# Two-head bias attention with a bilinear FFN: the tail keys' weighted values as 64-row matmuls, one accumulator bank per head

## The chip, the cores and the metric

The kernel runs on one core of a Trainium2 chip. The metric is the device time of one execution in microseconds (us); lower is better. A core has five engines that work on their own instruction streams and wait for each other by semaphores: TensorE (PE in the profile; its weight loads are listed apart as PEld), VectorE (DVE), ScalarE (ACT), GpSimd (POOL) and SyncE (SP). Here POOL and SP do little but issue DMAs.

## What is computed

```python
# q, k, v: (8 batches, 8 heads, 576 positions, 64), bias_table: (32, 8)
scores = q @ k.T / 8 + bias[head, |i - j| bucket]
attn   = softmax(scores)
x      = attn @ v              # heads side by side: (8 * 576, 512)
out    = ((x @ w_a) * (x @ w_b)) @ w_out     # 512 -> 1536 -> 512
```

In the kernel the bias enters as a factor: exp(score) is multiplied by exp(bias), and the sum of the weights comes out of the same matmul as the values, since v carries a column of ones (65 columns for a head).

## The kernel before

**Pairs.** The 64 heads of all batches are handled as 32 pairs of neighbouring heads; pair p belongs to batch p // 4. The 576 positions are split into 512 (four tiles of 128) and a tail of 64. So the two heads' tails of 64 make one tile of 128 rows: rows 0 to 63 for the first head, 64 to 127 for the second.

**Scores.** `qk` computes key tiles against queries, transposed (keys on the partitions): for each of four key tiles one bank-pair tile `qk` with both heads' 512 queries, as two matmuls of 64 rows (the head dimension), one for each head. They go in two groups, t = 0, 1 and t = 2, 3. With the second group come the "rows": all four key tiles against the 64 tail queries, 64-row and 64-column matmuls (L424), the first head into the bank `trb`, the second into a bank `qr` of the pool `ps_av`. `qk_tail` computes the tail keys against all queries (`qkt`). ACT takes the exponentials (`ex`, L439; `ex_rows`, L431; `ex_tail`, L515), VectorE multiplies with the bias factors (`mul`, L444; `mul_rows`, L539; `mul_tail`, L531). `mul_tail` writes the last 256 columns of the tail weights `att`: those of query tile 3 and of the tail queries (tile 4). For tail keys against query tiles 0 to 2 the factor is constant and drops out.

**Weighted values.** `av(p, jqs)` accumulates, for query tiles jq, into one bank `av` of the pool `ps_av`, a slot of 2 x 65 columns for each tile: first the tail keys of both heads in one matmul of 128 rows and 130 columns (L568; `vt` has zeros where a head meets the other head's rows), then four key tiles for each head (L578, 65 columns each). Tile 4 (the tail queries of both heads) instead takes four matmuls of 130 columns (L572). `av_norm` divides on VectorE (`rc`, L589; L591; L596) into `XG`. The calls are `av(p, (0, 1, 2))` and `av(p, (3, 4))`, one after the other through the same bank, and between them in most steps the row scores use that bank. `t_x` then transposes `XG` into `xn` by two DMAs on SP's queue (L604, L607).

**FFN.** Token chunks of 512 go through units: `pa` (four matmuls of 512 columns, then ACT copies to `ha`, L649), `pb` (four matmuls, then VectorE multiplies with `ha` into `g`, L652), and `po` (three units of four matmuls each, L679; then ACT copies to `ob`, L684, and issues the output DMA). The units take turns in two banks (`ps_ff`): a pa's bank is free when its `ha` is written, a pb's when its `g` is, a po's when its `ob` is. A chunk has 24 pa and pb units in turn and 12 of po.

**Order.** Everything is written out by hand; each engine runs its instructions in program order, and semaphores follow from what is read and written. After an opening that handles the pairs 0 to 7, a loop over s = 8 to 32 (the last function printed below) does the scores of pair s and the weighted values of pair s − 1. Its list `steps` is a sequence of these calls with places `U`; at each `U` one FFN unit is put, nine in a step. A chunk is 36 units, that is four steps: in steps with s mod 4 = 1 the units are pa, pb, ... pa; with s mod 4 = 2 pb, pa, ... pb; with s mod 4 = 3 six pa and pb and three po; with s mod 4 = 0 nine po. In steps with s mod 4 = 0 `av(p, (3, 4))` stands before the second score group (`late` before `pair`), in the others after it. Every step ends with `mul_tail(s)` behind the ninth unit. In step 32 the last pair's values are computed without scores, and the remaining units follow with two more banks.

PSUM has eight banks: four for scores (`ps_sc`, two tiles of two), one for `ps_av`, one for `trb`, two for the FFN. `trb` serves the transposes of the opening in two halves (`tr_half`).

Of the kernel before, what the change touches and what calls it, by code (L numbers as in the profile page):

```python
# [13 lines left out]
def kernel(  # L14
# [11 lines left out]
    nc = tc.nc  # L26
    FP32 = mybir.dt.float32
    BF16 = mybir.dt.bfloat16
    ACTF = mybir.ActivationFunctionType
    MULT = mybir.AluOpType.mult  # L30

    B, H, S, Dh = 8, 8, 576, 64
    NB = 32
    NM = 4
    SM = 128 * NM
    ST = S - SM
# [11 lines left out]
    wrk = ctx.enter_context(tc.tile_pool(name="wrk", bufs=2))  # L48
    atp = ctx.enter_context(tc.tile_pool(name="atp", bufs=10))
    ps_sc = ctx.enter_context(tc.tile_pool(name="ps_sc", bufs=2, space=bass.MemoryType.PSUM))  # L50
    ps_av = ctx.enter_context(tc.tile_pool(name="ps_av", bufs=1, space=bass.MemoryType.PSUM))
    ps_tr = ctx.enter_context(tc.tile_pool(name="ps_tr", bufs=1, space=bass.MemoryType.PSUM))
# [45 lines left out]
    vm = [wpool.tile([128, H, NM, Dh + 1], BF16, name=f"vm{i}") for i in range(2)]  # L98
    vt = [wpool.tile([128, 2, H // 2, Dh + 1], BF16, name=f"vt{i}") for i in range(2)]
# [8 lines left out]
    XG = [wpool.tile([128, 5, 2, Dh], BF16, name=f"XG{i}") for i in range(2)]  # L108
# [116 lines left out]
    def load_first(x, dst):  # L225
# [8 lines left out]
                        in_=bass.AP(tensor=bias_table.tensor, offset=(NB - 1) * H,  # L234
                                    ap=[[0, NB], [1, H]]))
# [5 lines left out]
                            op=mybir.AluOpType.subtract)  # L241
    warm = ps_av.tile([128, 512], FP32, tag="av", name="warm")

    def warm_up(n, dst=None):
        for _ in range(n):
# [7 lines left out]
                     start=True, stop=True)  # L253
# [54 lines left out]

    st = [dict() for _ in range(NP)]

    trb = ps_tr.tile([128, 1024], BF16, tag="tr", name="trb")
    turn = [0]

    def tr_half():
        turn[0] ^= 1
        return trb[:, 512 * turn[0]:512 * turn[0] + 512]

    def copy(eng, out, in_):
        if eng is nc.scalar:
# [88 lines left out]
    def qk(p, t0, ts=None):  # L408
        qT, kT, _ = operands(p)
        st[p].setdefault("at", [None] * NM)  # L410
        for t in ts or (t0, t0 + 1):
            ps = ps_sc.tile([128, 2, 512], FP32, tag="sc", name=f"qk{p}_{t}")
            for hh in range(2):
                r = slice(64 * hh, 64 * hh + 64)
                nc.tensor.matmul(out=ps[:, hh, :], lhsT=kT[r, t, :], rhs=qT[r, :, :],  # L415
                                 start=True, stop=True)
            st[p]["ps", t] = ps
        if shared(p) and t0 == 2:
            z = operands(p)[2]
            rows = (trb.bitcast(FP32), ps_av.tile([128, 512], FP32, tag="av", name=f"qr{p}"))  # L420
            for t in range(NM):
                for hh in range(2):
                    r = slice(64 * hh, 64 * hh + 64)
                    nc.tensor.matmul(out=rows[hh][:, ST * t:ST * t + ST], lhsT=kT[r, t, :],  # L424
                                     rhs=z[r, 0, ST * hh:ST * hh + ST], start=True, stop=True)
            st[p]["rows"] = rows
# [9 lines left out]
    def ex(p, t):  # L436
        ps = st[p]["ps", t]
        at = atp.tile([128, 2, SM], BF16, tag="at", name=f"at{p}_{t}")
        nc.scalar.activation(out=at[:, :, :], in_=ps[:, :, :], func=ACTF.Exp, scale=scale)  # L439
        st[p]["at"][t] = at  # L440

    def mul(p, t):
        at, w = st[p]["at"][t], W_sb[p % 4]
        nc.vector.tensor_tensor(out=at[:, :, :], in0=at[:, :, :],  # L444
                                in1=w[:, :, S - 1 + t:S - 1 + t - SM:-1], op=MULT)
# [95 lines left out]
    def weights(p, t, hh, jq):  # L541
        if p >= 4:
            return st[p]["at"][t][:, hh, 128 * jq:128 * jq + 128]
        o = 256 * (t % 2) + 128 * (jq % 2)
        return st[p]["at", jq // 2, t // 2][:, hh, o:o + 128]

    def weights_last(p, t):
        return st[p]["att"][:, 2 * ST * t:2 * ST * t + 2 * ST]

    def weights_tail(p, jq):  # L550
        if jq == 4:
            o = 512 + main_tail(p)
            return st[p]["att"][:, o:o + 2 * ST]
        if p < 4 and jq < 2:
            return atk[:, p, 128 * jq:128 * jq + 128]
        o = 512 + 128 * (jq if p >= 4 else jq - 2)
        return st[p]["att"][:, o:o + 128]

    def av(p, jqs):
        av_mm(p, jqs)  # L560
        av_norm(p, jqs)

    def av_mm(p, jqs, pool=None, tag="av"):
        b, hp = divmod(p, 4)
        i = b % 2
        pav = (pool or ps_av).tile([128, 3, 2, Dh + 1], FP32, tag=tag, name=f"av{p}_{jqs[0]}")
        for slot, jq in enumerate(jqs):
            nc.tensor.matmul(out=pav[:, slot, :, :], lhsT=weights_tail(p, jq),  # L568
                             rhs=vt[i][:, :, hp, :], start=True, stop=True)
            if jq == 4:  # L570
                for t in range(NM):
                    nc.tensor.matmul(out=pav[:, slot, :, :], lhsT=weights_last(p, t),  # L572
                                     rhs=vm[i][:, 2 * hp:2 * hp + 2, t, :], start=False,
                                     stop=True, skip_group_check=True)
                continue
            for hh in range(2):
                for t in range(NM):
                    nc.tensor.matmul(out=pav[:, slot, hh, :], lhsT=weights(p, t, hh, jq),  # L578
                                     rhs=vm[i][:, 2 * hp + hh, t, :], start=False,
                                     stop=True, skip_group_check=True)  # L580
        st[p]["pav", jqs[0]] = pav

    def av_norm(p, jqs):
        pav = st[p]["pav", jqs[0]]
# [15 lines left out]
    def t_x(p, jqs=range(5), eng=None):  # L600
        b, hp = divmod(p, 4)
        c0 = SM * B + ST * b
        if 4 <= p < NP - 1:
            nc.sync.dma_start_transpose(  # L604
                out=xn_sb[hp][:, SM * b:SM * b + SM].rearrange("d (j c) -> d j c", j=4),
                in_=XG[p % 2][:, 0:4, :, :].rearrange("p j h d -> p (j h d)"))
            nc.sync.dma_start_transpose(  # L607
                out=xn_sb[hp][:, c0:c0 + ST],
                in_=XG[p % 2][0:ST, 4, :, :].rearrange("p h d -> p (h d)"))
            return  # L610
        tr_x(p, jqs)
        copy_x(p, jqs, eng)
# [114 lines left out]
    def v_next(s):  # L727
# [11 lines left out]
        <wb0 <R2 <uq <q5 <q4 <R3 <k5 <wa1 <q7 <wb1 <k6 <uk <k7 <vb1a <vb1b <vt1a <q6 <wb2 <vt1b <wa2 <wo  # L739
        PC0:A PX0:D YQ0:A PC1:A PU0:D PV0:A PX1:D TQ0 YK0:D TK0 CQ00:A CQ01:D CK0:D TQ10 PF1:A CQ10:D  # L740
        S000 E000 PV1:D S001 E001 TK1 CK1:D TQ30 TZ1 CZ1:D S011 CQ30:D E011 S101 TQ20 CQ20:D E101 M101
# [126 lines left out]
    for s in range(8, NP + 1):  # L868
        new = s < NP
        U = "unit"  # L870
        A = lambda *jq: (lambda: av(s - 1, jq) if s > 8 else None)
        steps = []
        if new:
            steps += [lambda: (qk(s, 0), ex(s, 0))]
        if new:
            head = [U, lambda: ex(s, 1), A(0, 1, 2), U, lambda: mul(s, 0), U,
                    lambda: mul(s, 1)]
            late = [A(3, 4), lambda: t_x(s - 1), U]
            if s == 8:
                late = [U]  # L880
            pair = [lambda: v_next(s), lambda: (qk(s, 2), ex(s, 2), ex_rows(s)), U,
                    lambda: ex(s, 3), U, lambda: mul(s, 2), lambda: mul_rows(s)]
            tail = [lambda: (qk_tail(s), ex_tail(s)), U, U, lambda: mul_tail(s)]
            if s % 4 == 0:
                steps += head + late + [U] + pair + [lambda: mul(s, 3)] + tail
            else:
                steps += head + pair + late + [U, lambda: mul(s, 3)] + tail
        else:
            ff["late"] = True
            steps += [A(0, 1, 2), U, U, U, A(3, 4), lambda: t_x(s - 1, (0, 1, 2)), U, U, U,  # L890
                      lambda: t_x(s - 1, (3, 4)), U, U, U]
        b = s // 4 + 1
        if s % 4 == 2 and b < B:
            t_half(b, 0)
        if s % 4 == 0 and 2 <= b - 1 < B:
            t_half(b - 1, 1)
        if s % 4 == 1 and 2 <= b < B:
            load_vt(b)
        for bb in range(3, B):
            for g in range(2):  # L900
                if s == load_slot[bb] + (2 - (bb < 5)) * g:
                    load_half(bb, g)
        quota = 9
        seen, put = 0, 0
        nu = sum(1 for x in steps if x is U)
        for x in steps:
            if x is U:
                seen += 1
                n = (quota * seen + nu - 1) // nu - put
                put_units(n)  # L910
                put += n
            else:
                x()
# [31 lines left out]
```

## Time and profile before

| | |
|---|---|
| median of 3 runs | 413.51 us (412.92 to 413.57) |
| profiled execution, span | 412.1 us |
| TensorE busy | 401.5 us, 3420 matmuls recorded |
| VectorE busy | 240.6 us |
| ACT busy | 252.0 us |
| 128x65 value matmuls, L578 | 896 recorded, 41.2 us busy |
| 130-column tail matmuls, L568 | 152 recorded, 33.6 us busy |
| 130-column matmuls of tile 4, L572 | 128 recorded, 12.6 us busy |
| row scores, L424 | 96 for each head, 6.6 us busy each |

The profile is that of one execution, and its span runs from the first to the last instruction; the time of a run holds a little more. In a line of a group or of the timeline, `out<-in` are the tiles written and read, then rows*columns of the array for a matmul, the shapes, and how often. Matmuls are pipelined: one begins before the one ahead has ended, so what a matmul costs is the time to the next start, not its duration. Some matmul records are missing in a trace, so that a group of four sometimes shows three. In brackets stands how long the engine was idle before an instruction, and what released it.

### The profile page before, as it was taken

To read this page: it belongs to the slowest core of one execution; us is meant where nothing else is said; L and a number is where in the kernel's file an instruction comes from. 1 tells how busy PE (TensorE), PEld (TensorE's weight loads), DVE (VectorE), ACT (ScalarE), POOL (GpSimd) and SP (SyncE) were. 2 spreads that over 40 slices of the span, in tenths; PEclk is the share of its full clock that TensorE was granted. 3 is DMA by queue.
4 is the path that set the end of the run, shared out by engine and by line. 5 is a ranking of instruction groups with operands and counts; after the bars stand their busy time and mean duration, and the time that the engine had idled before them with its cause. 6 is when DMAs were issued, how large, how long until landed. Compare 5 with 4: busy or idle time off the path is not lost.

```text
span 412.1 us, 8718 instructions
## 1 busy us (share of the span) xinstructions
PE 401.5 (97%) x3420; PEld 209.6 (51%) x3471; DVE 240.6 (58%) x568; ACT 252.0 (61%) x386; POOL 131.4 (32%) x188
## 2 busy tenths in 40 slices
PE   7999999999999999999999999999999999999996
PEld 3476656455554555455445555555445454444443
DVE  4799997366755765476646764567547652421320
ACT  5898992577748665667557765767476642322321
POOL 5966466887029400960069004300000000000000
PEclk9999999999999999999999999999999999999999
DMA  9999999999969924994199908960520012002004
GB/s 152 185 204 197 206 137 148 166 184 131 91 127 157 141 40 91 151 127 94 35 159 150 120 17 136 117 92 17 117 67 17 16 40 78 0 5 98 2 2 102
DMA packets 135962, 42.36 MB, mean 103 GB/s; under 512 B 113544, under 2 KB 131176, under 8 KB 135920
## 3 DMA queue, kind: packets, MB, share of 16 engines
q0 software_dynamic: 81120, 19.88, 54.9%
q1 hardware_dynamic: 49456, 12.61, 19.9%
q10 hardware_dynamic: 5344, 9.31, 7.1%
q8 instruction: 27, 0.44, 0.5%
q14 instruction: 15, 0.12, 0.1%
HBM read 39.23 MB, written 9.45 MB: 118 GB/s over the span
## 4 chain that ended last, share of the span: by engine, by line
PE 95%; DMA 1%; ACT 1%; issue 1%; DVE 0%; ACTq 0%; SPq 0%
PE pb L642 23%; PE pa L642 23%; PE po L679 22%; PE av L578 8%; PE qk L415 7%; PE av L568 2%; PE av L572 2%; PE qkh L455 1%; PE qkt L488 1%; DMA xn<-in_k_dram 1%; PE trb L330 1%; PE trb L424 1%; PE trk L330 1%; ACT ath L461 0%; PE qkt L494 0%
## 5 line engine op out<-in xcount | busy, mean ns | idle before, releaser
L439 ACT ACTIVATE at<-qk 128x1024 bf16<-128x1024 f32 x112 | 113.4, 1029 | 27.4 <-DMA out_dram<-ob 10.3
L652 DVE TENSOR_TENSOR g<-pb,ha 128x512 bf16<-128x512 f32 (+1 forms) x114 | 75.6, 663 | 74.8 <-PE pb L642 58.5
L642 PE MATMUL pb<-xn,wb 128*128 128x512 bf16 (+1 forms) x440 | 111.1, 368 | 0.8
L642 PE MATMUL pa<-xn,wa 128*128 128x512 bf16 (+1 forms) x440 | 110.8, 368 | 0.7
L649 ACT ACTIVATE ha<-pa 128x512 f32<-128x512 f32 (+1 forms) x114 | 66.3, 581 | 67.6 <-PE pa L642 63.8
L679 PE MATMUL po<-wo,g 128*128 128x512 bf16 x403 | 95.5, 379 | 0.8
L444 DVE TENSOR_TENSOR at<-at,W 128x1024 bf16<-128x1024 bf16 x112 | 75.0, 685 | 22.4 <-ACT at L439 22.3
L642 PEld LDWEIGHTS <-wa 128*128 128x128 bf16 x456 | 41.2, 98 | 46.6 <-issue 6.8
L642 PEld LDWEIGHTS <-wb 128*128 128x128 bf16 x456 | 40.6, 98 | 42.9 <-issue 4.7
L679 PEld LDWEIGHTS <-g 128*128 128x128 bf16 x420 | 38.8, 98 | 44.9 <-issue 2.5
L684 ACT ACTIVATE ob<-po 128x512 f32<-128x512 f32 x34 | 20.4, 600 | 40.2 <-PE po L679 30.1
L578 PE MATMUL av<-vm,at 128*128 128x65 bf16 x896 | 41.2, 193 | 0.0
L578 PEld LDWEIGHTS <-at 128*128 128x128 bf16 x896 | 37.4, 97 | 6.1
L174 POOL DMA_DIRECT2D vt<-in_v_dram x12 | 7.4, 622 | 101.9 <-PE av L572 101.1
L136 POOL DMA_DIRECT2D qn<-in_q_dram x48 | 36.6, 825 | 9.2 <-PE trb L501 6.9
L589 DVE RECIPROCAL rc<-av 128x6 f32<-128x6 f32 (+1 forms) x64 | 11.9, 186 | 45.7 <-PE av L578 41.1
L145 POOL DMA_DIRECT2D kn<-in_k_dram x48 | 36.2, 800 | 2.6 <-DMA qn<-in_q_dram 1.6
L568 PE MATMUL av<-vt,att 128*128 128x130 bf16 x152 | 33.6, 221 | 0.2
L415 PE MATMUL qk<-QB,KB 64*128 64x512 bf16 x192 | 29.1, 381 | 0.3
L591 DVE TENSOR_TENSOR XG<-av,rc 128x384 bf16<-128x384 f32 (+2 forms) x64 | 27.2, 425 | 2.2
L515 ACT ACTIVATE att<-qkt 128x640 bf16<-128x640 f32 x24 | 16.8, 701 | 13.0 <-PE qkt L489 13.0
L568 PEld LDWEIGHTS <-att 128*128 128x128 bf16 x152 | 14.9, 98 | 6.4
(105 smaller groups left out, 322.8 us busy)
## 6 DMA issues: line engine op xcount, KB each, us to landing
out_dram<-ob ACTq DMA_DIRECT2D x31, 256.0 KB, 2.9
vn<-in_v_dram POOLq DMA_DIRECT2D x16, 256.0 KB, 5.7
kn<-in_k_dram POOLq DMA_DIRECT2D x48, 64.0 KB, 4.9
qn<-in_q_dram POOLq DMA_DIRECT2D x48, 64.0 KB, 4.1
wa<-in_moe_w_a_dram POOLq DMA_DIRECT2D x3, 512.0 KB, 8.9
wb<-in_moe_w_b_dram POOLq DMA_DIRECT2D x3, 512.0 KB, 8.3
wo<-in_moe_w_out_dram POOLq DMA_DIRECT2D x1, 1536.0 KB, 15.7
xn<-XG SPq DMA_TRANSPOSE x52, 3.5
```

The costliest lines, as they stand in the source:

```text
L136: nc.gpsimd.dma_start(out=by_tile(qn[b % 2])[:, h0 // 4, t, :, :], in_=q[b, h0:h1, 128 * t:128 * t + 128, :].transpose([1, 0, 2]))
L145: nc.gpsimd.dma_start(out=by_tile(kn[b % 2])[:, h0 // 4, t, :, :], in_=k[b, h0:h1, t:SM:NM, :].transpose([1, 0, 2]))
L415: nc.tensor.matmul(out=ps[:, hh, :], lhsT=kT[r, t, :], rhs=qT[r, :, :], start=True, stop=True)
L439: nc.scalar.activation(out=at[:, :, :], in_=ps[:, :, :], func=ACTF.Exp, scale=scale)
L444: nc.vector.tensor_tensor(out=at[:, :, :], in0=at[:, :, :], in1=w[:, :, S - 1 + t:S - 1 + t - SM:-1], op=MULT)
L568: nc.tensor.matmul(out=pav[:, slot, :, :], lhsT=weights_tail(p, jq), rhs=vt[i][:, :, hp, :], start=True, stop=True)
L578: nc.tensor.matmul(out=pav[:, slot, hh, :], lhsT=weights(p, t, hh, jq), rhs=vm[i][:, 2 * hp + hh, t, :], start=False, stop=True, skip_grou ...
L591: nc.vector.tensor_tensor(out=xg[:, jqs[0]:jqs[0] + m, :, :], in0=pav[:, 0:m, :, 0:Dh], in1=rc[:, 0:m, :].unsqueeze(3).to_broadcast([128, ...
L642: nc.tensor.matmul(out=ps[:, 0:n], lhsT=w[df // 4][:, mc, 128 * (df % 4):128 * (df % 4) + 128], rhs=xn_sb[mc][:, 512 * c + lo:512 * c + lo ...
L649: nc.scalar.activation(out=ha[:, 0:n], in_=ff["pa", df, lo][:, 0:n], func=ACTF.Copy)
L652: nc.vector.tensor_tensor(out=g_sb[df][:, lo:lo + n], in0=ff["pb", df, lo][:, 0:n], in1=ff["ha", df, lo][:, 0:n], op=MULT)
L679: nc.tensor.matmul(out=po[:, :], lhsT=g_sb[df][:, 128 * tt:128 * tt + 128], rhs=wo_sb[:, df, :], start=(df == 0), stop=(df == NDF - 1))
```

## The change

In steps 9 to 31 the weighted values of pair s − 1 (pairs 8 to 30) are no longer computed tile by tile but head by head, in two banks: one for each head, five query tiles of 65 columns in each.

- `av_tails(p)` starts both banks with the tail keys: for each of the five query tiles two matmuls of 64 rows and 65 columns, one for each head, into different banks. It stands directly behind the first score group `qk(s, 0)`, whose matmuls are of 64 rows too.
- `av_head(p, hh)` adds the four key tiles of one head: 20 matmuls of 128 rows and 65 columns. For tile 4 the weights are those of both heads' tail queries, and half of the result's rows is used. Head 0 stands behind the first unit of the step, head 1 behind the second.
- `norm_head(p, hh)` divides: a reciprocal of 5 columns, a multiply of four tiles, a multiply of the 64 tail rows, for each head.
- The two banks come from `two_banks`, for the values as for the row scores. The bank of `trb` is now handed out anew for each use instead of being held as one tile; a fresh `trz` is made for step 32.
- The steps all have one order now: `head`, `late` (a unit alone), `pair`, a unit with `mul(s, 3)`, `tail`. `t_x(s − 1)` stands behind the third unit.

```diff
-    trb = ps_tr.tile([128, 1024], BF16, tag="tr", name="trb")
+    trb = [ps_tr.tile([128, 1024], BF16, tag="tr", name="trb")]
...
+    def two_banks(name):
+        return (ps_tr.tile([128, 512], FP32, tag="tr", name=f"{name}_0"),
+                ps_av.tile([128, 512], FP32, tag="av", name=f"{name}_1"))
...
-            rows = (trb.bitcast(FP32), ps_av.tile([128, 512], FP32, tag="av", name=f"qr{p}"))
+            rows = two_banks(f"qr{p}")
...
+    J = Dh + 1
+
+    def av_tails(p):
+        b, hp = divmod(p, 4)
+        st[p]["av2"] = banks = two_banks(f"av{p}")
+        for jq in range(5):
+            for hh in range(2):
+                r = slice(64 * hh, 64 * hh + 64)
+                nc.tensor.matmul(out=banks[hh][:, J * jq:J * jq + J], lhsT=weights_tail(p, jq)[r, :],
+                                 rhs=vt[b % 2][r, hh, hp, :], start=(jq == 0), stop=True,
+                                 skip_group_check=True)
+
+    def av_head(p, hh):
+        b, hp = divmod(p, 4)
+        bank, v = st[p]["av2"][hh], vm[b % 2]
+
+        def mm(jq, t):
+            w = weights_last(p, t) if jq == 4 else weights(p, t, hh, jq)
+            return lambda: nc.tensor.matmul(out=bank[:, J * jq:J * jq + J], lhsT=w,
+                                            rhs=v[:, 2 * hp + hh, t, :], start=False, stop=True,
+                                            skip_group_check=True)
+
+        return [mm(jq, t) for jq in range(5) for t in range(NM)]
+
+    def norm_head(p, hh):
+        x = st[p]["av2"][hh][:, 0:5 * J].rearrange("p (j d) -> p j d", d=J)
+        rc = wrk.tile([128, 5], FP32, tag="rc2", name=f"rh{p}_{hh}")
+        nc.vector.reciprocal(out=rc[:, :], in_=x[:, :, Dh])
+        nc.vector.tensor_tensor(out=XG[p % 2][:, 0:4, hh, :], in0=x[:, 0:4, 0:Dh],
+                                in1=rc[:, 0:4].unsqueeze(2).to_broadcast([128, 4, Dh]), op=MULT)
+        rows = slice(ST * hh, ST * hh + ST)
+        nc.vector.tensor_tensor(out=XG[p % 2][0:ST, 4, hh, :], in0=x[rows, 4, 0:Dh],
+                                in1=rc[rows, 4:5].to_broadcast([ST, Dh]), op=MULT)
...
+        def AH(hh):
+            for put in (av_head(s - 1, hh) if s > 8 else ()):
+                put()
+            if s > 8:
+                norm_head(s - 1, hh)
         steps = []
         if new:
-            steps += [lambda: (qk(s, 0), ex(s, 0))]
+            steps += [lambda: (qk(s, 0), av_tails(s - 1) if s > 8 else None, ex(s, 0))]
         if new:
-            head = [U, lambda: ex(s, 1), A(0, 1, 2), U, lambda: mul(s, 0), U,
-                    lambda: mul(s, 1)]
-            late = [A(3, 4), lambda: t_x(s - 1), U]
-            if s == 8:
-                late = [U]
+            head = [U, lambda: ex(s, 1), lambda: AH(0), U, lambda: mul(s, 0), lambda: AH(1), U,
+                    lambda: (mul(s, 1), t_x(s - 1) if s > 8 else None)]
+            late = [U]
             pair = [lambda: v_next(s), lambda: (qk(s, 2), ex(s, 2), ex_rows(s)), U,
                     lambda: ex(s, 3), U, lambda: mul(s, 2), lambda: mul_rows(s)]
             tail = [lambda: (qk_tail(s), ex_tail(s)), U, U, lambda: mul_tail(s)]
-            if s % 4 == 0:
-                steps += head + late + [U] + pair + [lambda: mul(s, 3)] + tail
-            else:
-                steps += head + pair + late + [U, lambda: mul(s, 3)] + tail
+            steps += head + late + pair + [U, lambda: mul(s, 3)] + tail
         else:
             ff["late"] = True
+            trb[0] = ps_tr.tile([128, 1024], BF16, tag="tr", name="trz")
```

More of the change, by code (lines that the diff above doesn't have):

```diff
@@ L315, in tr_half @@
         turn[0] ^= 1
-        return trb[:, 512 * turn[0]:512 * turn[0] + 512]
+        return trb[0][:, 512 * turn[0]:512 * turn[0] + 512]
+    def two_banks(name):
+        return (ps_tr.tile([128, 512], FP32, tag="tr", name=f"{name}_0"),
+                ps_av.tile([128, 512], FP32, tag="av", name=f"{name}_1"))
     def copy(eng, out, in_):
```

## The prediction

> **What bounds the kernel now.** I read the page's first, second and fourth parts first.
>
> ```profile
> PE 401.5 (97%) x3420; PEld 209.6 (51%) x3471; DVE 240.6 (58%) x568; ACT 252.0 (61%) x386; POOL 131.4 (32%) x188
> ...
> PEclk9999999999999999999999999999999999999999
> ...
> PE 95%; DMA 1%; ACT 1%; issue 1%; DVE 0%; ACTq 0%; SPq 0%
> ```
>
> TensorE is busy 97% of the span, nowhere below nine tenths of its clock, and is 95% of the chain that ended last. The list of what TensorE waited for holds seven entries, all of them from the first 25 us; asked for 95 to 335 us alone, it is empty. The windows show how regular that part is: four steps of the loop at a time, five times (start and end, length, then busy time of PE, PEld, DVE, ACT and POOL with instructions, the granted clock, DMA share, GB/s).
>
> ```profile
> 98.36:142.38 44.02, 43.65 (x375) 22.28 (x382) 27.33 (x62) 29.12 (x44) 20.25 (x29) 1.00 1.22 129
> 142.38:186.40 44.02, 43.61 (x375) 22.27 (x382) 27.33 (x62) 29.12 (x44) 17.07 (x24) 1.00 0.93 107
> ```
>
> Both windows hold the same 375 matmuls and cover four steps exactly, whatever POOL and the DMAs do in them, so a step costs 11.0 us and is a sum of matmul times. A column saved on TensorE shortens the span one for one, and a new wait lengthens it the same way. The question is which is larger.
>
> **Price of the matmuls.** The time between starts in the timeline is what counts, since ends overlap (a 128x65 matmul "takes" 193 ns in its group, but 896 of them occupy 41.2 us).
>
> ```profile
> 236.28 1.03 PE L642 MATMUL pb<-xn,wb 128*128 128x512 bf16 x4
> 237.24 0.61 PE L415 MATMUL qk<-QB,KB 64*128 64x512 bf16 x4
> 237.78 1.04 PE L642 MATMUL pa<-xn,wa 128*128 128x512 bf16 x4
> 238.65 0.22 PE L568 MATMUL av<-vt,att 128*128 128x130 bf16 x1
> 238.72 0.42 PE L578 MATMUL av<-vm,at 128*128 128x65 bf16 x8
> 238.97 0.22 PE L568 MATMUL av<-vt,att 128*128 128x130 bf16 x1
> ```
>
> One 130-column and eight 65-column matmuls take 238.97 − 238.65 = 0.32 us. The 130-column one alone costs 0.058 us (the four of L572 and the one ahead of them run from 233.13 to 233.42 in the step before), which leaves 0.0323 for one of 65. An FFN unit (four of 512) costs 0.86 (234.28 to 235.15, where the next work starts).
>
> *Removed*, in each of 23 steps (s = 9 to 31): a block of three 130s and 24 65s (238.65 to 239.60, 0.95 us) and one of six 130s and eight 65s (232.81 to 233.42, 0.61 us): 1.56. *Added*: 40 matmuls of 65 columns, 40 × 0.0323 = 1.29, and ten tail matmuls of 64 rows. The nearest row for these is L424: 64 rows, 64 columns, heads alternating between the same two banks. Its pairs start at 230.86, 230.89, 230.92 and 230.95: 0.03 a pair. Five pairs: 0.15. New total 1.44, a saving of 0.12 a step, **2.8 us** over 23. Bounds: if the two heads did not overlap, 0.30 for the tails, and the step loses 0.03 (0.7 in all); if the tails vanished altogether, 0.27 saved (6.2). I take the pairs, because the row has the same rows, banks and alternation.
>
> The place matters for a second price. The score group starts 0.96 after the unit ahead of it, which costs 0.86: 0.10 goes where TensorE changes from 128-row to 64-row matmuls, and again where it changes back. Behind a score group the tails cost no further change; elsewhere they would cost 23 × 0.2 = 4.6 us.
>
> The Trainium skill says the same of the cause ("TensorEngine Tiling (Array Packing)", Key Properties: a change of tiling mode drains the engine). Another of its rules speaks against the change: "TensorE: Matmul & The Clock Gate", Back-to-back issue gap, gives a stream of weight loads and matmuls about 81 ns each at 128 columns. By that, nine more matmuls a step would be about 0.73 us, some 17 us in all, an estimate from that page; the rows above have 58 ns at 130 columns and 32 at 65, and the measurement decides.
>
> **What is added as a wait, first place.** The tails of query tiles 3 and 4 read columns that the multiply at L531 writes, the last VectorE instruction of the step before. Until now the first reader stood at least a unit later; now it stands right behind the score group. VectorE works in order, and at the end of a step s with s mod 4 = 2 the last unit is a pb, so its product (L652) is ahead of the multiply.
>
> ```profile
> 237.42 0.69 DVE L652 TENSOR_TENSOR g<-pb,ha 128x512 bf16<-128x512 f32 x1 [0.60 <-PE pb L642]
> 238.03 0.28 DVE L531 TENSOR_TENSOR att<-att,Wt 128x256 bf16<-128x256 bf16 x1
> ```
>
> The multiply ends at 238.31. The score group (two pairs of 0.216) lets the tails start at 237.24 + 0.43 = 237.67; three pairs later, at 237.76, TensorE wants tile 3. A woken TensorE starts 0.06 after its releaser (the copy of KT ends at 7.85 or just after, qkh starts at 7.92). So it stands still until 238.37: 0.61 us. Everything on TensorE queues behind it, first the next unit. Both ends of the delay hang on the same pb, so work moved elsewhere does not change it. It happens at six hand-overs (step 10 to 11, 14 to 15, ... 30 to 31): **3.7 us**. Bounds: 0.70 each if all ten tails wait for the multiply (4.2); zero if it is done in time, which nothing suggests. The other three kinds of hand-over pass: the multiply ends at 226.44 for a want at 226.75, at 247.65 for 248.76, and at 259.62 for 259.77; the last is late because ex(s, 3) is, and the new order puts a unit more between score group and tail scores there.
>
> **Second place: three units in a row.** The second block also was a cover. Until now it stood between the second score group and the tail scores (in three steps of four), so that nowhere more than two FFN units ran without other matmuls between. The new order is: scores and tails, unit 1, head 0, unit 2, head 1, units 3 and 4, scores, units 5, 6, 7, tail scores, units 8 and 9. The units share two banks; unit n+2 starts when the copy (ACT) or product (VectorE) of unit n is through.
>
> ```profile
> 230.85 1.02 ACT L439 ACTIVATE at<-qk 128x1024 bf16<-128x1024 f32 x1 [0.59 <-PE qk L415]
> 231.77 0.38 ACT L431 ACTIVATE att<-qr 128x256 bf16<-128x256 f32 x1
> 232.03 0.39 ACT L431 ACTIVATE att<-trb 128x256 bf16<-128x256 f32 x1
> 232.30 0.62 ACT L649 ACTIVATE ha<-pa 128x512 f32<-128x512 f32 x1
> ```
>
> After a second score group at 230.42 the copy ha of the unit behind it ends at 232.92, since the exponentials are ahead of it in ACT's queue: 2.50 after the group's start, 2.55 with the wake. The unit itself starts at 231.07, 0.65 after the group. For s mod 4 = 1 and 3, unit 5 is a pa, and unit 7 wants its bank at 0.65 + 2 × 0.8625 = 2.375 after the group. It is **0.17** late. For s mod 4 = 2, units 5 and 7 are pb: a product starts 1.13 after its unit (236.28 to 237.42), takes 0.69, wake 0.06: 1.88 against 1.725, **0.16** late; unit 8 then waits for a copy ready at about the same time and adds nothing. For s mod 4 = 0 all units are po, which hold a bank for three units: none. Six steps of each kind: 6 × (0.17 + 0.16 + 0.17) = **3.0 us**. Bounds: 0 (ACT and VectorE start a tenth or two earlier), and 0.30 each (5.4) if a queue is fuller than I see.
>
> **The rest** costs nothing. Normalising is six VectorE instructions as before, with two units to finish ahead of the second score group, which needs both banks back; by VectorE's queue it ends about 5 us after the first group starts, and the second follows at 5.5. If that cover were gone, the row scores and all behind them would wait. The transposing DMAs of t_x are issued some 3 us earlier in three steps of four and stand where they stood in the fourth (about 5.4 us into the step), the one whose output the next FFN chunk needs; SP's queue is free of the KB and QB transposes by then (250.8). In the steps that load tails they queue behind ZB<-tl (to 233.90), which still is before their old time of 235.16. POOL's load of vt, which waits for the last reader, goes a few us earlier. Pair 31 keeps the old code.
>
> **Sum.** 412.1 − 2.8 + 3.7 + 3.0 = 416.0. The median of the runs is 413.5, 1.4 above the profiled span, so 417.4, 0.9% slower.
>
> **Rivals.** *The saving alone* (faster): 412.1 − 2.8 + 1.4 = 410.7. One mechanism: the multiply is done when tile 3's tail comes up, and the units pass as well. For it: at 17 of 23 hand-overs it is done. Against: the product ahead of it in the queue waits for the very unit before the score group; it decides from 0.61 us of lateness down. *The tail wait alone*, with units 5 to 7 passing: 414.4. For it: 0.17 is the difference of long sums. Against: three rows agree on it. *Unpaired tails, or a third wait*: 23 × 0.15 = 3.4 more, 420.8. Against: L424's pairs.
>
> **How the numbers follow.** Forecast 0.62 (its own times 416.0 to 418.9), tail wait alone 0.16, saving alone 0.08, unpaired or more 0.14. Range 414.2 to 420.4: it takes in most of the second and part of the last. 0.2% is 0.8 us, about what this kernel's measurement can tell from no change: 412.7 to 414.3. Faster 0.08, same 0.08 (half of the tail wait alone), slower 0.84.
>
> **What would show it.** Right: a wait of TensorE's tail matmuls on L531 of about 0.6 us, six times; waits on L649 and L652 of 0.1 to 0.3 behind the second score group; four steps taking 44.02 − 4 × 0.12 + 0.61 + 0.50 = 44.65 us; tail pairs 0.03 apart. Wrong: no such waits and four steps in 43.5; starts evenly 0.03 apart for all ten tails; a wait on the normalising ahead of the row scores.

## The result, and the profile after

The changed kernel takes 418.5 us (median of 4 runs, 417.85 to 418.64) against 413.54 before: 1.0115 times, 95% interval 1.0101 to 1.013. Run again later beside other runs of the kernel before, it came to 1.0089 (1.0069 to 1.0109). The forecast of 417.4 is 1.0094 times the median that it started from.

The page of after, parts 1 and 4, and then what TensorE waited for (in total, times, the longest):

```profile
PE 400.4 (96%) x3618; PEld 209.5 (50%) x3678; DVE 242.7 (58%) x568; ACT 252.7 (61%) x386; POOL 131.6 (32%) x188
...
PE 89%; DVE 4%; issue 3%; ACT 2%; DMA 1%; ACTq 1%; SPq 0%; DVEq 0%
```

```profile
PE av L595 <- DVE att L535: 2.5, 6, 0.4
...
PE pa L680 <- ACT ha L687: 1.0, 5, 0.2
PE pb L680 <- DVE g L690: 1.0, 5, 0.2
```

TensorE has 198 recorded matmuls more and yet 1.1 us less busy time; the span is 416.7, 4.6 longer. VectorE and ACT have entered the chain of the work that ended last, and the list of waits, empty in the loop before, names both places of the prediction.

The windows from the first score group of step 9 to that of step 29, twenty steps, first before, then after:

```profile
83.17:303.27 220.10, 218.18 (x1868) 111.36 (x1902) 136.27 (x311) 145.59 (x221) 75.09 (x106) 1.00 0.95 108
```

```profile
83.53:306.31 222.78, 217.10 (x2042) 111.25 (x2082) 137.87 (x310) 146.16 (x220) 75.08 (x105) 1.00 0.93 107
```

These twenty steps take 2.68 us more, although there is less to do on TensorE in them. The hand-over from step 22 to 23 in the timeline of after, to lay beside the lines that the prediction shows:

```profile
239.24 0.61 PE L419 MATMUL qk<-QB,KB 64*128 64x512 bf16 x4
239.42 0.69 DVE L690 TENSOR_TENSOR g<-pb,ha 128x512 bf16<-128x512 f32 x1 [0.71 <-PE pb L680]
...
239.69 0.25 PE L595 MATMUL av<-vt,att 64*128 64x65 bf16 x6
240.03 0.28 DVE L535 TENSOR_TENSOR att<-att,Wt 128x256 bf16<-128x256 bf16 x1
240.37 0.23 PE L595 MATMUL av<-vt,att 64*128 64x65 bf16 x4 [0.42 <-DVE att L535]
240.53 0.39 PE L680 MATMUL pa<-xn,wa 128*128 128x512 bf16 x1
```

Six of the ten tail matmuls run at once, for query tiles 0 to 2; the other four wait for the multiply, which ends at 240.31, and start 0.06 later. The line says 0.42, but that counts from the modelled end of the sixth. Three pairs at 0.03 would have brought the fourth pair at about 239.78, so the loss is 0.585 us, as the single starts have it. It is the same in all six such steps. The unit behind the tails then comes 0.60 later than in the other steps (0.85 after the first tail instead of 0.25), and such a step takes 11.62 instead of 11.02.

The other place, in step 23, a few lines on in the same kernel:

```profile
245.37 0.61 PE L419 MATMUL qk<-QB,KB 64*128 64x512 bf16 x4
245.80 1.02 ACT L443 ACTIVATE at<-qk 128x1024 bf16<-128x1024 f32 x1 [0.59 <-PE qk L419]
...
246.72 0.65 ACT L435 ACTIVATE att<-qr 128x256 bf16<-128x256 f32 x2
246.90 1.03 PE L680 MATMUL pb<-xn,wb 128*128 128x512 bf16 x3
247.25 0.62 ACT L687 ACTIVATE ha<-pa 128x512 f32<-128x512 f32 x1
...
247.92 0.59 PE L717 MATMUL po<-wo,g 128*128 128x512 bf16 x2
```

The pb unit starts at 246.90 and costs 0.86, so the next is due at 247.76. It starts at 247.92, 0.05 after the copy `ha` ends (247.87). No idle time stands in brackets here: a matmul's modelled end lies 0.38 after its start, and a start put off from 0.216 to 0.37 leaves no gap. Eighteen steps lose 0.15 to 0.16 at this place; the list of waits shows ten of them, those where the record just ahead of the late unit is missing. In the second profile of the same kernel the list shows none, and the twenty steps take the same 222.78. A wait this short is read from starts. By the lengths of the steps it is 0.15 (11.02 with this wait, 10.88 in the steps without any).

In the steps with s mod 4 = 2 the late release is a product on VectorE, here in step 26:

```profile
278.96 1.04 PE L680 MATMUL pb<-xn,wb 128*128 128x512 bf16 x4
...
280.10 0.69 DVE L690 TENSOR_TENSOR g<-pb,ha 128x512 bf16<-128x512 f32 x1 [0.84 <-PE pb L680]
...
280.85 1.02 PE L680 MATMUL pb<-xn,wb 128*128 128x512 bf16 x4 [0.20 <-DVE g L690]
```

Two units after 278.96 the third is due at 280.69. The product of the first starts 1.14 after it and ends at 280.79, and the third unit starts 0.06 later.

So from step 9 to the last matmul the sum is 6 × 0.585 + 18 × 0.155 − 23 × 0.128 = 3.51 + 2.79 − 2.94 = 3.36, and the traces have 328.14 − 324.79 = 3.35 (from 83.53 to 411.67, and from 83.17 to 407.96). With 0.60 and 0.15, by the lengths of the steps, the sum is 3.36 too. The 0.128 is what a step is shorter by when nothing waits, from the experiments below. The remaining 1.3 of the span's 4.6 are 0.36 in the opening and 0.92 at the very end. The 0.36 is there at the first score group of step 8 already (74.08 for 73.72), ahead of all that the change touches; the first score group of step 9 comes between 82.9 and 83.8 in the ten profiles of all kernels, so this part is scatter.

The end: ACT's queue in the timeline of after, and then of before, from the copy of the last output tile but one.

```profile
409.27 0.60 ACT L722 ACTIVATE ob<-po 128x512 f32<-128x512 f32 x1 [1.99 <-PE po L717]
409.90 2.03 ACTq L729 DMA_DIRECT2D out_dram<-ob  x2
...
411.97 0.38 ACT L324 ACTIVATE ob_last<-po 128x256 f32<-128x256 f32 x1 [2.10 <-PE po L703]
```

```profile
405.56 0.60 ACT L684 ACTIVATE ob<-po 128x512 f32<-128x512 f32 x1 [1.99 <-PE po L679]
...
406.19 1.12 ACTq L691 DMA_DIRECT2D out_dram<-ob  x2
407.36 0.38 ACT L320 ACTIVATE ob_last<-po 128x256 f32<-128x256 f32 x1 [1.20 <-PE po L665]
```

Two output DMAs are issued in 2.03 us instead of 1.12, the second alone in 1.52 instead of 0.61, and the last copies queue behind it. Nothing in this part of the program changed. What stands beside it is a load of 16 KB of instructions (the queue of kind "instruction" in the page's third part, 29 loads instead of 27), from 410.34 to 411.55.

### The profile page after: what moved, and what is told of

The parts are those of the page before. It is cut to its first block, busy times and chain, and to the rows that moved or that the text cites. A ratio compares the mean times of both kernels' runs of the same rounds, so it can differ in the third digit from the quotient of the medians.

```text
span 416.7 us, 9150 instructions
## 1 busy us (share of the span) xinstructions
PE 400.4 (96%) x3618; PEld 209.5 (50%) x3678; DVE 242.7 (58%) x568; ACT 252.7 (61%) x386; POOL 131.6 (32%) x188
## 4 chain that ended last, share of the span: by engine, by line
PE 89%; DVE 4%; issue 3%; ACT 2%; DMA 1%; ACTq 1%; SPq 0%; DVEq 0%
PE po L717 22%; PE pb L680 22%; PE pa L680 21%; PE av L605 7%; PE qk L419 6%; PE av L582 2%; DVE g L690 2%; PE qkt L492 1%; PE qkh L459 1%; DMA xn<-in_k_dram 1%; PE av L595 1%; ACT ha L687 1%; PE av L572 1%; PE trb L334 1%; DVE ath L474 1%
## 5 line engine op out<-in xcount | busy, mean ns | idle before, releaser
L680 PE MATMUL pb<-xn,wb 128*128 128x512 bf16 (+1 forms) x428 | 108.6, 367 | 2.4 <-DVE g L690 1.0
L717 PE MATMUL po<-wo,g 128*128 128x512 bf16 x406 | 96.6, 379 | 0.8 <-issue 0.2
L448 DVE TENSOR_TENSOR at<-at,W 128x1024 bf16<-128x1024 bf16 x112 | 76.5, 686 | 11.9 <-ACT at L443 11.3
L680 PEld LDWEIGHTS <-wa 128*128 128x128 bf16 x456 | 40.1, 98 | 41.1 <-issue 3.8
L605 PEld LDWEIGHTS <-at 128*128 128x128 bf16 x736 | 29.6, 98 | 10.9
L614 DVE RECIPROCAL rh<-av 128x5 f32<-128x5 f32 x46 | 8.8, 192 | 44.2 <-PE av L605 43.0
L605 PE MATMUL av<-vm,at 128*128 128x65 bf16 x736 | 31.0, 194 | 0.1
L615 DVE TENSOR_TENSOR XG<-av,rh 128x256 bf16<-128x256 f32 x46 | 19.5, 425 | 1.6
L465 ACT ACTIVATE ath<-qkh 128x1024 bf16<-128x1024 f32 x16 | 15.8, 1024 | 3.0 <-PE qkh L459 2.9
L435 ACT ACTIVATE att<-qr 128x256 bf16<-128x256 f32 x48 | 15.8, 387 | 0.0
```

Source lines behind the costliest of these rows:

```text
L448: nc.vector.tensor_tensor(out=at[:, :, :], in0=at[:, :, :], in1=w[:, :, S - 1 + t:S - 1 + t - SM:-1], op=MULT)
L605: return lambda: nc.tensor.matmul(out=bank[:, J * jq:J * jq + J], lhsT=w, rhs=v[:, 2 * hp + hh, t, :], start=False, stop=True, skip_group_ ...
L615: nc.vector.tensor_tensor(out=XG[p % 2][:, 0:4, hh, :], in0=x[:, 0:4, 0:Dh], in1=rc[:, 0:4].unsqueeze(2).to_broadcast([128, 4, Dh]), op=MULT)
L680: nc.tensor.matmul(out=ps[:, 0:n], lhsT=w[df // 4][:, mc, 128 * (df % 4):128 * (df % 4) + 128], rhs=xn_sb[mc][:, 512 * c + lo:512 * c + lo ...
L717: nc.tensor.matmul(out=po[:, :], lhsT=g_sb[df][:, 128 * tt:128 * tt + 128], rhs=wo_sb[:, df, :], start=(df == 0), stop=(df == NDF - 1))
```

## The experiments

Each run was measured beside runs of the kernel before on the same chip (medians 414.19 for the first four, 413.91 for the others); ratios are against those. The lines of the code quoted are those of the changed kernel.

**The multiply one unit earlier**

```diff
-            tail = [lambda: (qk_tail(s), ex_tail(s)), U, U, lambda: mul_tail(s)]
+            tail = [lambda: (qk_tail(s), ex_tail(s)), U, lambda: mul_tail(s), U]
```

> Only the multiply of the tail weights (L535) is issued one unit earlier, between the eighth and the ninth unit, so that no product of the last pb stands ahead of it. Theory (the tail matmuls wait for the multiply in six steps, 0.585 us each by the trace of after): these six waits go, 6 x 0.585 = 3.5 us, and nothing takes their place: 418.5 - 3.5 = 415.0. The waits of the seventh unit (about 0.155 us) stay as they are. Rival (the wait only gives the other engines time that they need anyway; without it the next wait for a copy or a product moves up): 417 or more, and new waits at L680.

414.36 us, ratio 1.0008 (0.9994 to 1.0022), where 415.0 was expected; the profiled span, 413.2, is the expected 3.5 below after. The twenty steps take 219.81, 2.97 below after, for five of the six waits: 0.59 each. The timeline of this kernel at the same hand-over:

```profile
236.90 0.28 DVE L535 TENSOR_TENSOR att<-att,Wt 128x256 bf16<-128x256 bf16 x1
237.51 0.61 PE L419 MATMUL qk<-QB,KB 64*128 64x512 bf16 x4
237.68 0.69 DVE L690 TENSOR_TENSOR g<-pb,ha 128x512 bf16<-128x512 f32 x1 [0.51 <-PE pb L680]
...
237.95 0.31 PE L595 MATMUL av<-vt,att 64*128 64x65 bf16 x10
238.20 0.39 PE L680 MATMUL pa<-xn,wa 128*128 128x512 bf16 x1
```

The multiply now lies ahead of the product and is done before the score group starts; the ten tails run through, and the unit behind them starts 0.25 after the first of them. The order of two instructions on VectorE was the whole wait. The rival falls: no wait moved up in its place.

**The row exponentials behind the copy**

```diff
-            pair = [lambda: v_next(s), lambda: (qk(s, 2), ex(s, 2), ex_rows(s)), U,
-                    lambda: ex(s, 3), U, lambda: mul(s, 2), lambda: mul_rows(s)]
+            pair = [lambda: v_next(s), lambda: (qk(s, 2), ex(s, 2)), U,
+                    lambda: (ex_rows(s), ex(s, 3)), U, lambda: mul(s, 2), lambda: mul_rows(s)]
```

> Only the two exponentials of the row scores (L435) are moved in ACT's order, behind the copy ha of the fifth unit. Theory (in steps with s mod 4 = 1 and 3 the seventh unit waits for a bank whose copy stands behind three exponentials in ACT's queue): the copy ends about 0.13 us earlier, limited then by its own matmuls, and of 0.155 us in twelve steps about 0.03 is left: 418.5 - 1.5 = 417.0. The waits in the steps with s mod 4 = 2 (a product on VectorE) and the six waits on the multiply stay. Rival (the seventh unit waits for something else, as for the bank itself or the array): no change, 418.5.

416.69 us, ratio 1.0055 (1.0039 to 1.0071), where 1.0115 and 1.0089 were measured for the changed kernel. The twenty steps take 221.26, 1.52 below after, over ten of these places: 0.15 each, so nothing of the wait is left where 0.03 was expected. In the timeline of this kernel, in step 23:

```profile
245.88 1.03 PE L680 MATMUL pb<-xn,wb 128*128 128x512 bf16 x3
246.08 0.60 ACT L687 ACTIVATE ha<-pa 128x512 f32<-128x512 f32 x1 [0.27 <-PE pa L680]
246.57 0.66 ACT L435 ACTIVATE att<-qr 128x256 bf16<-128x256 f32 x2
246.74 0.59 PE L717 MATMUL po<-wo,g 128*128 128x512 bf16 x2
```

The copy now waits for its own matmuls (0.27 in brackets), ends at 246.68, and the seventh unit starts when it is due, 0.86 after the pb. So it was ACT's queue. The six waits on the multiply stay, and the steps with s mod 4 = 2 still lose theirs to the product on VectorE, as both were meant to.

**The tails of one head after the other**

```diff
-        for jq in range(5):
-            for hh in range(2):
+        for hh in range(2):
+            for jq in range(5):
```

with the early multiply.

> As e1, and the ten tail matmuls in another order: all five of the first head, then all five of the second, so that neighbours use the same rows and the same bank. Theory (two 64-row matmuls overlap only when the one behind uses the other rows): starts evenly 0.03 us apart, ten for 0.30 instead of 0.15: 23 x 0.15 = 3.4 us more than e1, 418.4. Rival (the array takes both heads in any order, or the weight loads set the pace): as e1, 415.0.

415.46 us, ratio 1.0034 (1.0021 to 1.0047): neither theory. The twenty steps take 220.70, 0.045 a step above the run with the early multiply, not 0.15 and not 0. The tails of step 23 in its timeline:

```profile
238.75 0.36 PE L595 MATMUL av<-vt,att 64*128 64x65 bf16 x10
239.04 0.39 PE L680 MATMUL pa<-xn,wa 128*128 128x512 bf16 x1
```

From the first tail to the next unit it is 0.29, against 0.25 with the heads in turn. One behind the other the ten would take 0.30, and 0.09 for the change of rows comes on top. The single starts (238.751, .780, .788, .812, .827, .842, .862, .871, .892, .921) look like two streams, each some 0.03 apart, the second one begun 0.037 after the first. Which head they belong to shows in six of the 23 steps, where the records of the two heads' first tails each carry a semaphore wait. With the heads in turn these two waits stand on the first and the second of the ten; here the same two stand on the first and the third, 0.037 apart, though in the program the second head's first tail is the sixth. So the two heads overlap although the program does not alternate them. The Trainium skill, "TensorE: Matmul & The Clock Gate", The mechanism, says that matmuls start and end strictly in program order; five of one head and then five of the other, kept in order, could overlap only where they meet, and the measured 0.29 does not fit that.

**The tails among 128-row matmuls**

```diff
-            steps += [lambda: (qk(s, 0), av_tails(s - 1) if s > 8 else None, ex(s, 0))]
+            steps += [lambda: (qk(s, 0), ex(s, 0))]
...
-            head = [U, lambda: ex(s, 1), lambda: AH(0), U, lambda: mul(s, 0), lambda: AH(1), U,
+            head = [U, lambda: ex(s, 1), lambda: av_tails(s - 1) if s > 8 else None, lambda: AH(0), U, lambda: mul(s, 0), lambda: AH(1), U,
```

with the early multiply.

> As e1, but the ten tail matmuls stand behind the first FFN unit, ahead of head 0, among matmuls of 128 rows. Theory (each change between 64-row and 128-row matmuls costs TensorE about 0.095 us, and behind the score group the tails cost no further one): two more changes in 23 steps, 23 x 0.19 = 4.4 us more than e1, 419.4. Rival (the changes are hidden by the weight loads of such short matmuls): as e1, 415.0.

419.51 us, ratio 1.0128 (1.0109 to 1.0147), 5.15 above the run with the early multiply. The twenty steps take 224.04, 4.23 above it: 0.21 a step, 4.9 for 23. The timeline of step 22:

```profile
229.81 0.81 PE L680 MATMUL pb<-xn,wb 128*128 128x512 bf16 x3
230.56 0.33 PE L595 MATMUL av<-vt,att 64*128 64x65 bf16 x10
230.81 0.69 PE L605 MATMUL av<-vm,at 128*128 128x65 bf16 x16
```

The last of the pb's matmuls starts at 230.24 (its end, 229.81 + 0.81, less the 0.38 that one takes) and costs 0.216; the tails start at 230.56, 0.1 late, and the head's matmuls again 0.1 after the tails are through. The place behind the score group is worth more than the saving in columns: without it the change would lose even with the wait gone.

**The changed kernel again, and the load of instructions moved.** The first is the changed kernel as it is; the second has

```diff
-    warm_up(5)
+    for _ in range(25):
+        nc.tensor.matmul(out=warm[:, 0:102], lhsT=zero_sb[:, 0:128], rhs=zero_sb[:, 0:102],
+                         start=True, stop=True)
```

> The changed kernel once more, as a measure for the other runs on the same chip: 1.0115 times before, 5 us more. Both theories of the end (see the run with more short warm-up matmuls) expect the last DMA issue of L729 at 1.3 to 1.7 us again.

> The changed kernel, with the five warm-up matmuls of 512 columns at the very start as 25 of 102 columns: the same columns, 40 TensorE instructions more (weight loads and matmuls). Theory (at the end of the changed kernel the last block of TensorE's instructions is loaded just when ACT issues its last output DMA but two, which then takes 1.5 us instead of 0.6 and holds up the last copies; the block falls there because the kernel has 414 more TensorE instructions): the load comes 20 matmuls, 4.3 us, earlier, the issue takes 0.6 us, and the time is 0.9 us below the changed kernel. Rival (the long issue belongs to the DMA queue or to the kernel's end and not to the load): it stays at 1.3 to 1.7 us, and the time with it.

1.0089 (1.0069 to 1.0109) and 1.0074 (1.0056 to 1.0092): by the times alone the two are not told apart (0.6 between the medians, 0.9 expected). By the traces they are. The changed kernel's second profile has the long issue again (1.38 us, with a load from 409.79 to 410.75). With the load moved, 406.55 to 407.95, the two issues take what they took before (line numbers are two higher in this kernel):

```profile
409.84 1.12 ACTq L731 DMA_DIRECT2D out_dram<-ob  x2
411.01 0.39 ACT L326 ACTIVATE ob_last<-po 128x256 f32<-128x256 f32 x1 [1.20 <-PE po L705]
```

From the start of the last matmul to the end of the span it is 4.2 us here and was 4.15 before the change, 5.07 and 4.93 in the two profiles of after. So in the traces moving the load by 40 instructions takes the 0.8 us away. The ten profiles show besides when a lengthened issue ends: each of the six long ones ends 0.37 to 0.38 after the end of the load beside it. So does the second of the two issues beside the moved load (407.66 to 408.32, 0.66 instead of 0.61). Why an issue waits for the load is open: the one ahead of it (407.15, 0.47) lies wholly inside the load and takes its usual time, and in the loop issues that overlap a load take the usual 0.34.

**Without the waits.** Early multiply, row exponentials late in the odd steps, and for s mod 4 = 2 another order:

```diff
...
+            if s % 4 == 2:
+                steps += [U, lambda: ex(s, 1), U, lambda: AH(0), U, lambda: mul(s, 0), lambda: AH(1), U,
+                          lambda: (mul(s, 1), t_x(s - 1)), U, lambda: v_next(s),
+                          lambda: (qk(s, 2), ex(s, 2), ex_rows(s)), U, lambda: ex(s, 3),
+                          lambda: mul(s, 2), lambda: mul_rows(s), U, lambda: mul(s, 3)] + tail
...
```

> The changed kernel with the early multiply of e1, the late row exponentials of e2 in the odd steps, and in steps with s mod 4 = 2 another place for one unit: two ahead of head 0, two between head 1 and the second score group, two behind it, so that no three stand in a row. Theory (nothing but these waits stood against the saving): TensorE waits for nothing in the loop, a step is 0.13 us shorter than before, 23 x 0.13 = 3.0 us; the end keeps its 0.9: 2 us below before, ratio 0.995. Rival (with the waits gone ACT or VectorE, at 60% on average, hold up the score tiles in some step): waits at L419 or L680, and no gain over e1, ratio 1.000.

> e3 with the warm-up matmuls of the run on the moved load: another 0.9 us below e3 if that theory holds, ratio 0.993; as e3, 0.995, if the rival does.

411.85 us, ratio 0.9944 (0.9925 to 0.9962), and with the moved load 410.62, 0.9917 (0.9898 to 0.9936). Both beat the kernel before. The window of the twenty steps of the first:

```profile
83.08:300.62 217.54, 217.54 (x2083) 111.05 (x2082) 138.74 (x310) 145.84 (x220) 76.98 (x108) 1.00 0.96 111
```

TensorE is busy for the whole window and waits for nothing in the loop. 220.10 − 217.54 = 2.56 in twenty steps is the change's own saving, 0.128 a step. The two intervals overlap, so that the moved load helps here too is likely and not shown by the times; in the traces the stretch from the last matmul to the end is 4.5 and 4.1. In the first of the two the load (404.26 to 405.21) begins when the last issue of L729 is over, which took its usual 0.61, and the next issue, at L710, is held in its place: 0.86 instead of 0.50, to 0.39 after the load's end.

## Why the prediction was right, point by point

- **What bounds.** TensorE was the sum of its matmuls, so both a saving and a wait went to the span in full. The run without waits shows the first, the run with the early multiply the second.
- **The saving**, forecast at 0.12 a step and 2.8 us: measured 0.128 and 2.9.
- **The tail wait**, forecast at 0.61 in six steps, 3.7 us: measured 0.585 to 0.60, 3.5 to 3.6. It begins at the fourth pair as worked out, since the first three read columns that the multiply does not write.
- **Three units in a row**, forecast at 0.17, 0.16 and 0.17 in six steps each, 3.0 us: measured 0.15 to 0.16 in all three kinds, 2.7 to 2.8. That ACT's queue made it in the odd steps is shown by the moved exponentials; for the steps with s mod 4 = 2 the trace has the product's end 0.06 ahead of the late unit, and the order without three in a row removed it.
- **"The rest costs nothing"** failed: about 0.9 at the end, in a part that the change leaves alone. The prediction counted TensorE's instructions as time on TensorE only; 414 more also move the places where their code is loaded. The loop came out 0.55 below its sum (3.35 for 3.9), the end 0.9 and the opening 0.36 above it, which makes the span's 4.6; the medians differ by 5.0, and the time is 1.1 above the forecast, inside the range. These errors have opposite signs, and the opening is scatter, so that the time came this near is in part luck; the sum for the loop is not.
- **The rival of unpaired tails** was priced at 0.15 a step and fell: in the changed kernel the pairs start 0.03 apart. The run with the heads one after the other shows 0.045, so without the waits even that order would have saved 0.08 a step.
- **What was to show it** did: the six waits, the short waits behind the second score group, tail pairs 0.03 apart, four steps in 44.56 (44.65 forecast).

## What to carry to other kernels

Where one engine is a gapless sum, moving work next to like work can save its columns and still lose: ask of each moved instruction what it reads, which engine writes that last, and what stands ahead of that write in its queue. A reordering that leaves three users of two buffers in a row has taken away a cover, and that is seen by comparing the release time of one buffer with the time of two units. Here the cure was to issue one write a unit earlier, one pair of reads later, and one unit at another place.

## What the runs showed of the hardware that was not expected

- Two 64-row matmul streams in different banks overlap without being alternated in the program: 0.29 us to the next unit for ten in two runs of five, 0.25 for ten in turn, where in series it would be 0.39.
- A load of instructions lengthened the kernel's end: a DMA issue on ACT's queue took 1.3 to 1.7 us instead of 0.61 in the six profiles where a 16 KB load began within 0.15 us of its start, and 0.61 to 0.62 in the four where it did not. In all six the issue ended 0.37 to 0.38 after the load. 414 more TensorE instructions had moved the load there, and 40 more moved it away.
